# The last quad of a sliding-window attention step, its values loaded in two pieces in place of four

## The chip, the core and the metric

The kernel runs on one core of a Trainium2 chip. The metric is the device time of one execution in microseconds; three runs of the kernel before gave 186.46, 186.56 and 186.88, median 186.56.

## What is computed

One decoding step of attention for 32 sequences (B = 32, one token each). 32 query heads share 8 key/value heads (4 each), the head size is 128, and only the last 512 positions of a cache of 2048 are looked at. All inputs are bf16.

```
q = (x @ wq)                                  # 32 x 512 by 512 x 4096
k, v = last 512 rows of each cache, per (batch, kv head)
scores = q . k * 128**-0.5 ; p = softmax(scores)
o = p . v                                     # per (batch, head)
out = o.reshape(32, 4096) @ wo                # 4096 x 512
```

The keys and the values that are read are 33.5 MB each, wq and wo 4.2 MB each: 75.5 MB in all.

## The kernel before

**Tiling.** The batch is cut into eight quads of four sequences (q = 0 to 7). A quad's keys are one tile of 128 partitions by 32 KB: a partition is one (sequence, kv head, quarter of the window), its row 128 cache rows on end. The values of a quad have the same shape. There are two buffers each, `K_sb` and `V_sb`, used in turn by even and odd quads. At the start `V_sb[1]` holds wq; at the end `K_sb[0]` holds wo.

**Steps of a quad.** The texts `PE_OPS`, `DVE_OPS` and `ACT_OPS` (lines 19 to 33) give each engine its order of work by hand, one word for each step, and `needs` (lines 89 to 118) says what each step waits for. T turns the keys (VectorE, `KT_sb`, line 445); S makes the scores (TensorE, line 331); M, X and N are the softmax (VectorE and ScalarE); E brings the probabilities into the order of the value rows (TensorE, line 346) and G copies them out; B spreads them into a block-diagonal tile `bd` (ScalarE line 509, VectorE line 465). P multiplies by the values (TensorE, line 361): 32 groups of 4 matmuls, each group reading 512 columns of `V_sb`. `P7.0.32` in the order is all 32 groups of quad 7. C copies its result (VectorE line 470, ScalarE line 514), F folds it (line 373) and D writes it into `o_sel` (line 518). P of a quad waits for C of the quad before, F for C of its own. The end of TensorE's order is P6, F5, P7, F6, F7, and after D7 the projection by wo (line 393) in three blocks, one for each piece W0, W1, W2 of wo (16, 12 and 4 row groups); two copies each on VectorE and ScalarE and one store finish.

**Loads.** All large loads are issued by SyncE (SP) on one queue, in the order of the text `LOADS` (lines 35 to 37): K is a quad's keys in one piece, `Vq.i` is piece i of a quad's values, W the pieces of wo. `V_PIECES` (line 40) says into how many pieces the values of each quad are cut: 1 for quads 0 to 4, 2 for quads 5 and 6, 4 for quad 7. A piece takes its share of every partition's row, so whole tiles come in rows of 32 KB, halves in rows of 16 KB, quarters in rows of 8 KB. Each piece has a semaphore of its own. SP waits before the first piece of a quad's values (line 233) until P of the quad two before has ended, since it writes that buffer; the next pieces then follow without a wait. On TensorE `v_waits` (lines 178 to 184) puts a wait for a piece before the first group that reads it.

The lines that set this:

```
n = R // V_PIECES[q]                                  # line 234, R = 128
r0 = op[2] * n
sp.dma_start(V_sb[q % 2][:, r0 * DH:(r0 + n) * DH], rows(v_cache, q, r0, r0 + n)
...
n = V_PIECES[q]                                       # line 180, in v_waits
for i in range(n):
    if g0 <= i * 32 // n < g1:
        c = sum(1 for p in range(q % 2, q + 1, 2) if V_PIECES[p] > i)
        yield i * 32 // n, sem_v[q % 2][i], 16 * c
```

Of the kernel before, what the change touches and what calls it, by code (L numbers as in the profile page):

```python
# [32 lines left out]
"""  # L33

LOADS = """
K0 K1 V0.0 K2 V1.0 K3 V2.0 K4 V3.0 K5 K6 V4.0 K7 V5.0 V5.1 V6.0 V6.1 V7.0 V7.1 V7.2 V7.3 W0 W1 W2
""".split()

X_PARTS = [(0, 2), (2, 8), (8, 18), (18, 32)]
V_PIECES = [1, 1, 1, 1, 1, 2, 2, 4]  # L40
WOP = [(0, 16), (16, 28), (28, 32)]


# [4 lines left out]
def bass_standalone__sliding_block_cached__sampling_kernel(  # L48
# [71 lines left out]
    with ExitStack() as es:  # L120
# [46 lines left out]
        sem_k = [sem(f"sem_k{i}") for i in range(2)]  # L167
        sem_v = [[sem(f"sem_v{i}_{j}") for j in range(max(V_PIECES))] for i in range(2)]
        sem_wo = [sem(f"sem_wo{i}") for i in range(len(WOP))]
# [8 lines left out]
        def v_waits(q, g0, g1):  # L178

            n = V_PIECES[q]  # L180
# [4 lines that stand above are left out]
# [34 lines left out]
        def _(sp):  # L219
# [3 lines left out]
            for op in ops_of(" ".join(LOADS)):  # L223
# [5 lines left out]
                elif kind == "V":  # L229
                    if q == 1:  # L230
                        sp.wait_ge(s["pe_q"], 8)
                    if q >= 2:
                        wait([ends["P", q - 2, 31]])
                    n = R // V_PIECES[q]
                    r0 = op[2] * n
# [323 lines left out]
```

## Time and profile before

| what | us |
|---|---|
| median of three runs (186.46 to 186.88) | 186.56 |
| the profiled execution: its own time | 186.74 |
| its span, first to last instruction | 185.0 |
| TensorE busy with matmuls | 119.9 |
| VectorE busy | 106.5 |
| ScalarE busy | 49.7 |

The mean granted TensorE clock was 0.825 of full speed. The profile is of one execution. "Busy" is the time in which an engine had an instruction in work; "landing" is when a load's semaphore shows that all its bytes are there. All loads together moved 75.5 MB at a mean of 409 GB/s over the span. In the chain of waits each step is put down to what released the next, followed back from the end. In rows of the timeline the first two numbers are start and duration in us, x is the number of instructions, and the bracket gives the idle time of the engine before and what ended it.

### The profile page before, as it was taken

To read this page: it belongs to the slowest core of one execution; us is meant where nothing else is said; L and a number is where in the kernel's file an instruction comes from. 1 tells how busy PE (TensorE), PEld (TensorE's weight loads), DVE (VectorE), ACT (ScalarE), POOL (GpSimd) and SP (SyncE) were. 2 spreads that over 40 slices of the span, in tenths; PEclk is the share of its full clock that TensorE was granted. 3 is DMA by queue.
4 is the path that set the end of the run, shared out by engine and by line. 5 is a ranking of instruction groups with operands and counts; after the bars stand their busy time and mean duration, and the time that the engine had idled before them with its cause. 6 is when DMAs were issued, how large, how long until landed. Compare 5 with 4: busy or idle time off the path is not lost.

```text
span 185.0 us, 3664 instructions
## 1 busy us (share of the span) xinstructions
PE 119.9 (65%) x1636; PEld 56.3 (30%) x1636; DVE 106.5 (58%) x106; ACT 49.7 (27%) x93; POOL 16.9 (9%) x52
## 2 busy tenths in 40 slices
PE   0089104447696597649934994342799899898943
PEld 0024000013453153314421351001345446354542
DVE  0031999994549524972298328999637996320201
ACT  3000300012925037301650154001062715420301
POOL 7900040202000110001000200020000000000000
PEclk9999965556999799687995599655569999999996
DMA  6998999999999999999999999999999999999960
GB/s 213 421 500 369 432 454 454 454 390 404 450 454 443 411 386 454 454 436 425 392 436 454 432 418 411 439 446 439 418 411 411 429 425 425 411 420 431 431 287 27
DMA packets 3872, 75.80 MB, mean 410 GB/s; under 512 B 464, under 2 KB 528, under 8 KB 656
## 3 DMA queue, kind: packets, MB, share of 16 engines
q1 hardware_dynamic: 3792, 75.53, 95.9%
q8 instruction: 13, 0.21, 0.5%
q10 hardware_dynamic: 64, 0.03, 0.1%
q14 instruction: 3, 0.02, 0.0%
HBM read 75.53 MB, written 0.03 MB: 409 GB/s over the span
## 4 chain that ended last, share of the span: by engine, by line
DMA 59%; DVE 22%; PE 9%; issue 6%; SPq 2%; ACTq 1%; DVEq 0%
DMA K_sb<-in_k_cache_dram 43%; DVE KT_sb L445 17%; DMA K_sb<-in_wo_dram 12%; PE ps L313 4%; PE ps L361 4%; DMA bd<-in_x_dram 4%; DVE QT_sb L437 2%; DVE KT_sb L434 1%; SPq L236 1%; DVE C_sb L470 1%; ACTq L187 1%; SPq L242 1%; PE ps L331 1%; DVE bd L413 0%; PE ps L393 0%
## 5 line engine op out<-in xcount | busy, mean ns | idle before, releaser
L445 DVE STREAM_TRANSPOSE KT_sb<-K_sb 128x4096 f32<-128x4096 f32 x16 | 70.5, 4431 | 9.7 <-DMA K_sb<-in_k_cache_dram 9.6
L361 PE MATMUL ps<-V_sb,bd 32*128 32x512 bf16 x1024 | 64.1, 402 | 4.3 <-DMA V_sb<-in_v_cache_dram 1.7
L331 PE MATMUL ps<-KT_sb,QBD 128*32 128x512 bf16 x256 | 26.0, 544 | 39.0 <-DVE KT_sb L445 29.8
L361 PEld LDWEIGHTS ps<-V_sb,bd 32*128 32x128 bf16 x1024 | 27.4, 98 | 38.3 <-issue 14.7
L331 PEld LDWEIGHTS ps<-KT_sb,QBD 128*32 128x32 bf16 x256 | 6.7, 115 | 55.6 <-DVE KT_sb L445 36.9
L496 ACT ACTIVATE P_f<-ps,negmax 128x512 f32<-128x512 f32 x8 | 5.5, 687 | 62.3 <-DVE negmax L453 62.3
L509 ACT ACTIVATE bd<-PTc,mask 128x512 bf16<-128x512 bf16 x31 | 20.1, 711 | 0.3
L514 ACT ACTIVATE C_sb<-ps 32x512 f32<-32x512 f32 x22 | 12.9, 587 | 23.7 <-PE ps L361 23.5
L289 POOL COPY QBD<-QT_sb 32x128 bf16<-32x128 bf16 x32 | 9.2, 287 | 106.6 <-PE ps L331 89.9
L465 DVE TENSOR_SCALAR bd<-PTc,mask 128x512 bf16<-128x512 bf16 x33 | 9.3, 348 | 15.3 <-ACT PTc L503 15.3
L470 DVE COPY C_sb<-ps 32x512 f32<-32x512 f32 x10 | 6.9, 693 | 14.5 <-PE ps L361 14.4
L373 PE MATMUL ps<-C_sb,F_sb 128*128 128x128 f32 x64 | 9.7, 298 | 5.6 <-ACT C_sb L514 5.0
L373 PEld LDWEIGHTS ps<-C_sb,F_sb 128*128 128x128 f32 x64 | 8.2, 200 | 8.4 <-ACT C_sb L514 7.2
L346 PE MATMUL ps<-P_bf,E_sb 128*128 128x128 bf16 x128 | 9.8, 237 | 1.1 <-DVE P_bf L459 1.1
L451 DVE TENSOR_REDUCE maxv<-ps 128x1 f32<-128x512 f32 x8 | 5.5, 687 | 8.4 <-PE ps L331 8.4
L503 ACT ACTIVATE PTc<-ps 128x512 bf16<-128x512 f32 x8 | 4.7, 593 | 19.6 <-PE ps L346 19.6
L346 PEld LDWEIGHTS ps<-P_bf,E_sb 128*128 128x128 bf16 x128 | 8.3, 107 | 5.1 <-DVE P_bf L459 2.5
L313 PE MATMUL ps<-V_sb,bd 128*128 128x512 bf16 x32 | 9.1, 453 | 0.8 <-DVE bd L413 0.8
L301 PE MATMUL ps<-bd 32*128 32x128 bf16 x4 | 0.6, 295 | 8.9 <-DMA bd<-in_x_dram 8.9
L434 DVE CAST KT_sb<-ps 128x512 bf16<-128x512 f32 x4 | 2.5, 682 | 6.5 <-PE ps L313 6.5
L413 DVE CAST bd<-ps 128x512 bf16<-128x512 f32 x1 | 0.7, 692 | 9.5 <-PE ps L301 9.5
L490 ACT ACTIVATE KT_sb<-ps 128x512 bf16<-128x512 f32 x4 | 2.1, 603 | 14.3 <-PE ps L313 14.3
(29 smaller groups left out, 34.3 us busy)
## 6 DMA issues: line engine op xcount, KB each, us to landing
K_sb<-in_k_cache_dram SPq DMA_DIRECT2D x8, 4096.0 KB, 25.6
V_sb<-in_v_cache_dram SPq DMA_DIRECT2D x5, 4096.0 KB, 29.4
V_sb<-in_v_cache_dram SPq DMA_DIRECT2D x4, 2048.0 KB, 20.2
V_sb<-in_wq_dram SPq DMA_DIRECT2D x2, 2048.0 KB, 9.8
V_sb<-in_v_cache_dram SPq DMA_DIRECT2D x4, 1024.0 KB, 11.8
K_sb<-in_wo_dram SPq DMA_DIRECT2D x1, 2048.0 KB, 18.8
K_sb<-in_wo_dram SPq DMA_DIRECT2D x1, 1536.0 KB, 21.8
K_sb<-in_wo_dram SPq DMA_DIRECT2D x1, 512.0 KB, 22.6
```

The lines of the kernel that those rows point to most:

```text
L289: pool.tensor_copy(QBD[pr, q % 2].rearrange("p (w t) (h c) -> p w t h c", w=2, h=HKV)[:, :, :, :, 4 * b:4 * b + 4], QT_sb[pr, q].rearrange ...
L313: ins = pe.matmul(ps[:, n], lhsT=xT_sb[:, kt, :], rhs=wq_sb[:, kt, n * 512:(n + 1) * 512], start=kt == 0, stop=kt == DKT - 1, tile_positio ...
L331: ins = pe.matmul(S_ps[32 * c:32 * c + 32, :], lhsT=QBD[:, q % 2, 2 * w + t, c0:c0 + 32], rhs=KT_sb[:, w, :, KB * h:KB * h + KB, t], start ...
L346: ins = pe.matmul(EP_ps[:, e * R:(e + 1) * R], lhsT=E_sb[:, k, e].rearrange("p m j -> p (m j)"), rhs=P_bf[:, k * R:(k + 1) * R], start=k = ...
L361: ins = pe.matmul(O_ps[:, b, :], lhsT=bd[pr, q % 2, 4 * g:4 * g + 4].rearrange("p r h e -> p (r h e)"), rhs=V_sb[q % 2][pr, 512 * g:512 * ...
L373: ins = pe.matmul(F_ps[:, 0:P], lhsT=F_sb[:, d].rearrange("p h d -> p (h d)"), rhs=C_sb[:, q % 2, :, 32 * d:32 * d + 32], start=d == 0, st ...
L445: return dve.transpose(KT_sb[:, w].bitcast(F32).rearrange("p r c t -> p r (c t)"), K_sb[q % 2][:, :].bitcast(F32).rearrange("p (r w c) -> ...
L451: dve.tensor_reduce(maxv[:, q:q + 1], S_ps, AX.X, ALU.max).then_inc(s["dve_m"], 1)
L465: ins = dve.tensor_scalar(o, i, m, None, op0=ALU.mult)
L470: ins = dve.tensor_copy(*pick_args(q, r))
L509: ins = act.activation(o, i, ACTF.Copy, scale=m)
L514: ins = act.activation(*pick_args(q, r), ACTF.Copy)
```

## The change

The values of the last quad come in two pieces in place of four: `V_PIECES` ends in 2, and the words V7.2 and V7.3 leave the order of the loads. SP issues two DMAs of 2 MB (rows of 16 KB) where it issued four of 1 MB (rows of 8 KB). P7 has a wait before groups 0 and 16 where it had one before groups 0, 8, 16 and 24. As `sem_v` is made for the largest entry of `V_PIECES`, each of the two value buffers has two semaphores in place of four. All else is the same.

```
 LOADS = """
-K0 K1 V0.0 K2 V1.0 K3 V2.0 K4 V3.0 K5 K6 V4.0 K7 V5.0 V5.1 V6.0 V6.1 V7.0 V7.1 V7.2 V7.3 W0 W1 W2
+K0 K1 V0.0 K2 V1.0 K3 V2.0 K4 V3.0 K5 K6 V4.0 K7 V5.0 V5.1 V6.0 V6.1 V7.0 V7.1 W0 W1 W2
 """.split()
...
-V_PIECES = [1, 1, 1, 1, 1, 2, 2, 4]
+V_PIECES = [1, 1, 1, 1, 1, 2, 2, 2]
```

## The prediction

> **What bounds the kernel now.** I read the page first, its parts 1 to 3, to see which engine is full.
>
> ```profile
> span 185.0 us, 3664 instructions
> PE 119.9 (65%) x1636; PEld 56.3 (30%) x1636; DVE 106.5 (58%) x106; ACT 49.7 (27%) x93; POOL 16.9 (9%) x52
> DMA  6998999999999999999999999999999999999960
> ...
> q1 hardware_dynamic: 3792, 75.53, 95.9%
> q8 instruction: 13, 0.21, 0.5%
> ```
>
> No compute engine is above 65%; the 16 DMA engines are full from the second slice to the last but one. The kernel is a stream of 75.5 MB, and the end is set by when its last byte lands and by what must follow. So the next view is the end of the chain of waits (start, duration, what), and beside it the end of the timeline.
>
> ```profile
> 155.47 0.54 SPq L236
> 156.00 0.04 issue
> 156.04 0.60 SPq L236
> ...
> 158.62 0.43 SPq L242
> 159.05 0.04 issue
> 159.09 22.60 DMA K_sb<-in_wo_dram
> 181.69 0.04 issue
> ```
>
> ```profile
> 161.73 3.63 PE L361 MATMUL ps<-V_sb,bd 32*128 32x512 bf16 x64 [0.80 <-DMA V_sb<-in_v_cache_dram]
> 165.42 1.40 DVE L470 COPY C_sb<-ps 32x512 f32<-32x512 f32 x2 [6.70 <-PE ps L361]
> 167.07 7.09 PE L361 MATMUL ps<-V_sb,bd 32*128 32x512 bf16 x128 [0.62 <-DVE C_sb L470]
> 174.21 1.40 DVE L470 COPY C_sb<-ps 32x512 f32<-32x512 f32 x2 [7.39 <-PE ps L361]
> ...
> 177.33 1.08 PE L393 MATMUL ps<-K_sb,o_sel 128*32 128x128 bf16 x64 [0.37 <-ACT o_sel L518]
> 180.50 0.85 PE L393 MATMUL ps<-K_sb,o_sel 128*32 128x128 bf16 x48 [2.09 <-DMA K_sb<-in_wo_dram]
> 181.74 0.64 PE L393 MATMUL ps<-K_sb,o_sel 128*32 128x128 bf16 x16 [0.38 <-DMA K_sb<-in_wo_dram]
> ```
>
> The reader is to see three things. The last piece of wo (W2) lands at 181.69 and the last 16 matmuls start 0.05 later: this landing sets the end, with 3.3 us of fixed tail behind it (185.0 - 181.7). TensorE runs the value matmuls of the last quad (P7) from 167.07 without a break, started by the copy of P6 (165.42 + 1.40 = 166.82) and not by a load. And after the first block of the output projection, at 178.41, TensorE idles 2.09 us until W1 lands: the compute path has spare time there.
>
> Last, the landings. The semaphore events of the trace date them: V5.0 145.75, V5.1 150.65, V6.0 156.79, V6.1 161.69, V7.0 164.46, V7.1 166.94, V7.2 169.40, V7.3 171.90, W0 176.79, W1 180.46, W2 181.69. The view of DMA issues, asked for the issue at 155.47, the one at 157.34 and W0's at 157.98, and the stage sums say the same more coarsely:
>
> ```profile
> V_sb<-in_v_cache_dram SPq DMA_DIRECT2D x1, 1024.0 KB, 9.0
> V_sb<-in_v_cache_dram SPq DMA_DIRECT2D x1, 1024.0 KB, 14.6
> K_sb<-in_wo_dram SPq DMA_DIRECT2D x1, 2048.0 KB, 18.8
> ```
>
> ```profile
> 141.00:158.00 17.00, 16.40 (x268) 8.80 (x264) 14.76 (x17) 7.84 (x15) 0.00 (x0) 1.00 1.00 423
> 161.30:168.10 6.80, 5.75 (x92) 3.16 (x96) 1.39 (x2) 1.45 (x3) 0.00 (x0) 1.00 1.01 418
> ```
>
> The last columns are the granted clock, the DMA share and GB/s. In the first stretch only 16 KB rows move, in the second only 8 KB rows; both keep the engines full.
>
> **The change, part by part.** Everything up to 155.47, when SP's wait for P5 ends and V7.0 is issued, is untouched, so only the tail is costed.
>
> *Row size.* Two pieces of 16 KB rows replace four of 8 KB rows, the same 4 MB. Clean steps between landings: 2.48 and 2.46 and 2.50 us for 1 MB in 8 KB rows (164.46 to 171.90), mean 2.48; 4.90, 4.90 and 4.89 us for 2 MB in 16 KB rows (V5.0 to V5.1, V6.0 to V6.1, V7.3 to W0). So 4 x 2.48 = 9.92 becomes 2 x 4.90 = 9.80: -0.12. The rates agree: 4.194 MB take 10.03 us at 418 GB/s and 9.92 at 423, -0.11. Everything queued behind (W0, W1, W2) lands 0.12 earlier, as does the second half of V7 (171.78).
>
> *Two DMA issues fewer on SP.* Each took 0.60 us and 0.04 between: W0 to W2 are issued 1.28 us sooner. Costed at nothing: W0 is issued at 157.98, but followed packet by packet no DMA engine ends V7.3 before 168.15, so the issue has 10 us of cover. Nothing else is queued on SP until the output store. Were that cover gone the change would gain up to 1.28.
>
> *Two semaphore waits fewer in P7 on TensorE.* P7 waited at groups 0, 8, 16 and 24 and now waits at 0 and 16. None of the four showed idle time; 0.
>
> *The wait that becomes coarser.* First half: all 2 MB have to be there before group 0. They land where V7.1 did, 166.94 less half of 0.12, so 166.88, while P7 is held anyway until 167.07. About 0. Second half: group 16 is reached at 167.07 + 7.09/2 = 170.6 and its piece lands at 171.78, so TensorE waits 1.2 us; before, groups 16 and 24 needed their pieces at 170.6 and 172.4 and had them at 169.40 and 171.90. Behind this wait stand, on TensorE, 64 matmuls, two folds and the projection; on DVE and ACT the copies of P7. P6's second half shows the price: released by a landing at 161.69, started at 161.73, its copies begin 3.69 later. So the copies of P7 begin at 171.82 + 3.69 = 175.51 in place of 174.21: 1.30 late. The rest of that path shifts by as much: the projection's first block starts at 178.63 and ends at 179.71. W1 lands at 180.46 - 0.12 = 180.34: 0.63 still idle. If the path slipped further, W1's block of 0.85 would have to end by W2's landing at 181.57, so the first block could end at 180.72: the path is covered up to a slip of 1.01 more. Taken: 0. Bounds: below, the path cannot gain; above, 64 matmuls at half clock. The trace has 32 such matmuls in 3.44 us at a granted 0.50 (120 to 130), so 64 take 6.9 and not 3.63: +3.25, less the cover of 1.01, is +2.2. I take 0 since the granted clock was 1.00 from 137 to 181.6, through waits of 0.80 and 0.62.
>
> *The last 16 matmuls.* They took 0.64 for the clock fell to half at 181.57. At full clock, by the rows of 64 in 1.08 and 48 in 0.85 (0.0144 each), 16 take 0.39. With the change TensorE idles 0.63 and not 2.09 us shortly before, so the fall may not come: between 0 and -0.25. I take 0, because nothing says where the clock's steps fall in another run.
>
> The Trainium skill, "TensorE: Matmul & The Clock Gate", section Part 1, says that the clock is halved after an idle stretch judged in free-running windows of 3.4 us. By it the shorter idle time could spare the fall, and the sum would be -0.37 instead of -0.12. The trace's steps lie on a grid of 3.41 us, which agrees, but it shows one phase of that grid only.
>
> Sum: -0.12 + 0 + 0 + 0 + 0 = -0.12. The profiled execution took 186.74 (span 185.0 and 1.7 around it), 0.18 over the median of 186.56; it becomes 186.6, and the median **186.4**.
>
> **Rivals.** The runs before lie from 186.46 to 186.88; 0.2%, or 0.37 us, is about what can be told from no change.
>
> *B, the last block stays at full clock:* -0.12 - 0.25 = -0.37, 186.2. For it: the shorter idle time. Against it: it needs the median run to have had the fall before. It sits on the bound of 0.37.
>
> *C, the issues do count:* the chain of waits puts all four issues of V7 on the path. Two fewer and the shorter stream: -0.12 - 1.28 = -1.40, 185.2. Against it: W0 lands 4.89 after V7.3, a full engine's pace, so no engine waited for the issue.
>
> The Trainium skill, "DMA: Bandwidth & Descriptors", section Anatomy of one DMA, gives about 2 us fixed for each DMA plus its bytes at 436 GB/s, fitted on another path of issue; two DMAs fewer would be worth 4.0 us there, 182.6 by that estimate. The steps of 2.48 for 1 MB leave no room for a fixed 2 us between queued DMAs, so the trace does not agree.
>
> *D, slower, the coarse wait decides:* P7's second half comes more than 1.01 + 1.30 later than now, and then every further microsecond is one of the end. The price goes from 0 to the +2.2 above: 186.5 to 188.6. For it: two thirds of the present 2.09 us of idle time are used up. Against it: every duration in the sum is a measured row at the same clock.
>
> *E, slower, an instruction fetch more on the slowest engine:* V6.0 landed 6.14 after V5.1, not 4.90, since a 16 KB instruction packet (one of the 13 on q8) ran on that engine at 151.1. Followed packet by packet, one engine took 4.02 us over a megabyte in place of 2.48 when it was hit at 160.9, so a fetch costs its engine 1.5. At W2 four engines land 1.2 us or more behind the other twelve, and the last of them is the landing that counts. One fetch more on it: 186.4 + 1.5 = 187.9. Against it: the last four fetches before W2 (151.1, 160.9, 167.1, 175.7) each made another engine late and none a late one later, and TensorE's matmuls stay the same.
>
> **How the numbers follow.** Forecast 0.50, B 0.24, C 0.10, D 0.11, E 0.05. The forecast's own range is 186.2 to 186.7 (0 to -0.37, and the runs' spread). Outside the range stand C, E and D's upper half, 0.20 in all: it goes from 185.9 (B with the spread below) to 186.9 (D's lower part). Faster: C 0.10, two thirds of B 0.16, and 0.06 of the forecast, 0.32. Slower: D 0.10, E 0.05, 0.15. Within 0.2%: 0.53.
>
> **What would show it.** Right: V7.0 landing near 166.9 and V7.1 near 171.8; P7 in two blocks of 64 matmuls with an idle 1.2 us charged to the load of V between them; the wait before W1's block down from 2.09 to about 0.6; W2 landing near 181.6. Wrong: no wait before W1's or W2's block (D); landings of W0 to W2 earlier by about a microsecond (C); W2 later by 1.5 with P7 as forecast (E); the last block at 0.4 in place of 0.64 (B).

## The result, and the profile after

The changed kernel takes 186.44 us (median of 20 executions, 186.21 to 186.81). The kernel before, run beside it 20 times, takes 186.88 (186.46 to 187.59), 0.3 more than in the three runs shown ahead of the prediction. The ratio (its time over that of the kernel before beside it) is 0.9974, 95% interval 0.9964 to 0.9984: faster by 0.49 us, 0.30 to 0.67. The forecast was 186.4 and a gain of 0.12. The time and the sign came out, but the gain was four times the forecast; the rest of it lies in the spread of the kernel before.

The page of the changed kernel, parts 1 to 3 and the end of its chain of waits (start, duration, what):

```profile
span 184.7 us, 3662 instructions
...
DMA  6999999999999999999999999999999999999970
...
q1 hardware_dynamic: 3504, 75.53, 95.9%
```

```profile
155.66 0.54 SPq L236
156.20 0.04 issue
156.24 0.60 SPq L236
...
157.95 0.04 issue
157.99 23.64 DMA K_sb<-in_wo_dram
181.64 0.04 issue
```

Two issues fewer stand in the chain. The wait for W2 begins 1.1 us sooner (157.99, where it was 159.09), and W2 lands at 181.64, where it was 181.69: the earlier issue bought nothing, as the wait grew from 22.60 to 23.64. The timeline of the changed kernel's tail (start, duration, engine, operation; in brackets the idle time before it and what ended it; only the rows of the value matmuls and of the projection):

```profile
162.08 3.63 PE L361 MATMUL ps<-V_sb,bd 32*128 32x512 bf16 x64 [0.96 <-DMA V_sb<-in_v_cache_dram]
167.42 3.63 PE L361 MATMUL ps<-V_sb,bd 32*128 32x512 bf16 x64 [0.61 <-DVE C_sb L470]
171.88 3.63 PE L361 MATMUL ps<-V_sb,bd 32*128 32x512 bf16 x64 [0.83 <-DMA V_sb<-in_v_cache_dram]
...
178.69 1.08 PE L393 MATMUL ps<-K_sb,o_sel 128*32 128x128 bf16 x64 [0.37 <-ACT o_sel L518]
180.45 0.85 PE L393 MATMUL ps<-K_sb,o_sel 128*32 128x128 bf16 x48 [0.68 <-DMA K_sb<-in_wo_dram]
181.68 0.43 PE L393 MATMUL ps<-K_sb,o_sel 128*32 128x128 bf16 x16 [0.37 <-DMA K_sb<-in_wo_dram]
```

P7 is now two blocks of 64 matmuls. The second waits for its half of V7, the projection starts at 178.69 in place of 177.33, and the idle time before W1's block has shrunk from 2.09 to 0.68 us. The last block took 0.43 and not 0.64, as the clock fell only at 184.17 in this execution and at 181.57 in the profile before.

The stage sums over the same stretches as before show the rows (last column GB/s):

```profile
141.00:158.00 17.00, 15.96 (x260) 8.64 (x256) 14.64 (x16) 7.64 (x14) 0.00 (x0) 1.00 1.01 426
161.30:168.10 6.80, 5.40 (x88) 2.95 (x92) 1.39 (x2) 1.45 (x3) 0.00 (x0) 1.00 1.00 424
```

The second stretch moved 8 KB rows at 418 GB/s before and moves 16 KB rows at 424 now.

### The profile page after: what moved, and what is told of

The parts are those of the page before. It is cut to its first block, busy times and chain, and to the rows that moved or that the text cites. A ratio compares the mean times of both kernels' runs of the same rounds, so it can differ in the third digit from the quotient of the medians.

```text
span 184.7 us, 3662 instructions
## 1 busy us (share of the span) xinstructions
PE 119.1 (65%) x1636; PEld 56.8 (31%) x1636; DVE 106.6 (58%) x106; ACT 49.8 (27%) x93; POOL 16.9 (9%) x52
## 4 chain that ended last, share of the span: by engine, by line
DMA 77%; DVE 13%; issue 3%; PE 3%; SPq 3%; DVEq 0%
DMA K_sb<-in_k_cache_dram 49%; DMA V_sb<-in_v_cache_dram 15%; DMA K_sb<-in_wo_dram 13%; DVE KT_sb L445 12%; PE ps L361 2%; SPq L236 1%; SPq L228 1%; SPq L242 1%; PE ps L331 1%; SPq L193 0%; DVE C_sb L470 0%; DVE maxv L451 0%; PE ps L393 0%; DVEq L120 0%; DVE P_bf L479 0%
## 5 line engine op out<-in xcount | busy, mean ns | idle before, releaser
L361 PE MATMUL ps<-V_sb,bd 32*128 32x512 bf16 x1024 | 63.1, 397 | 4.7 <-DMA V_sb<-in_v_cache_dram 2.9
L331 PE MATMUL ps<-KT_sb,QBD 128*32 128x512 bf16 x256 | 25.3, 532 | 39.7 <-DVE KT_sb L445 30.0
L346 PE MATMUL ps<-P_bf,E_sb 128*128 128x128 bf16 x128 | 11.0, 255 | 0.8 <-DVE P_bf L459 0.8
L346 PEld LDWEIGHTS ps<-P_bf,E_sb 128*128 128x128 bf16 x128 | 9.3, 116 | 4.9 <-DVE P_bf L459 2.8
L313 PE MATMUL ps<-V_sb,bd 128*128 128x512 bf16 x32 | 8.5, 433 | 0.8 <-DVE bd L413 0.8
```

The costliest lines, as they stand in the source:

```text
L313: ins = pe.matmul(ps[:, n], lhsT=xT_sb[:, kt, :], rhs=wq_sb[:, kt, n * 512:(n + 1) * 512], start=kt == 0, stop=kt == DKT - 1, tile_positio ...
L331: ins = pe.matmul(S_ps[32 * c:32 * c + 32, :], lhsT=QBD[:, q % 2, 2 * w + t, c0:c0 + 32], rhs=KT_sb[:, w, :, KB * h:KB * h + KB, t], start ...
L346: ins = pe.matmul(EP_ps[:, e * R:(e + 1) * R], lhsT=E_sb[:, k, e].rearrange("p m j -> p (m j)"), rhs=P_bf[:, k * R:(k + 1) * R], start=k = ...
L361: ins = pe.matmul(O_ps[:, b, :], lhsT=bd[pr, q % 2, 4 * g:4 * g + 4].rearrange("p r h e -> p (r h e)"), rhs=V_sb[q % 2][pr, 512 * g:512 * ...
```

## The experiments

Two theories stood against each other at first. *Row theory:* all of the gain is the price of 8 KB rows and of two DMAs. *Clock theory:* 0.14 is that price, and the rest comes because TensorE's work lies 1.3 us later, idles less before W1, and keeps its clock for the last blocks. Every kernel was timed against the kernel before on the same chip; the experiments ran on three chips.

### The changed kernel again

Edit: none.

> The changed kernel itself, run beside the kernel before on the same chip as the next three. Both theories: about 0.4 to 0.5 us faster than before (20 runs gave 186.44 against 186.88). Clock theory: its times lie close together (within about 0.5 us), those of the kernel before spread by a microsecond, as the clock falls early, late or not at all in the 2.1 us in which TensorE idles before the second block of the projection.

Measured: 186.40 (12 executions, 186.27 to 186.55), the kernel before 186.67 (35 executions, 186.31 to 187.60), ratio 0.9985 (0.9974 to 0.9995). A gain of 0.28 by the ratio: just under the lower end of the first one, and less than the 0.4 to 0.5 that both theories expected. The spreads are as the clock theory said: the changed kernel's twelve lie within 0.3 us. Of the 35 of the kernel before, 26 lie from 186.31 to 186.80 and nine from 187.15 to 187.60, with nothing between. I call the latter *late* (187.0 or more).

### Only TensorE's timing changed

```diff
 # pv(): with four pieces of V7 as before
-pieces = {g: (sm, n) for g, sm, n in v_waits(q, g0, g1)}
+for g, sm, n in v_waits(q, g0, g1):   # quad 7: pieces 0, 1 before group 0; 2, 3 before group 16
+    pieces.setdefault(g - g % 16 if q == NQ - 1 else g, []).append((sm, n))
```

> The kernel before with four pieces of V7 and 8 KB rows kept, but P7 waits for its pieces as the changed kernel does: pieces 0 and 1 before group 0, pieces 2 and 3 before group 16. TensorE's work is moved later by 1.3 us and nothing else changes. Clock theory: 0.25 to 0.35 us faster than before, that is the gain less the 0.14 of the stream; the wait before the second block of the projection goes from 2.1 to about 0.7 us. Row theory: no change, within 0.1 us, or slower.

Its timeline:

```profile
171.81 3.63 PE L363 MATMUL ps<-V_sb,bd 32*128 32x512 bf16 x64 [1.04 <-DMA V_sb<-in_v_cache_dram]
...
180.28 0.85 PE L395 MATMUL ps<-K_sb,o_sel 128*32 128x128 bf16 x48 [0.58 <-DMA K_sb<-in_wo_dram]
181.51 0.43 PE L395 MATMUL ps<-K_sb,o_sel 128*32 128x128 bf16 x16 [0.38 <-DMA K_sb<-in_wo_dram]
```

Measured: 186.55 (12 executions, 186.30 to 186.70), ratio 0.9990 (0.9979 to 1.0000). A gain of 0.12 by the medians and 0.19 by the ratio, where 0.25 to 0.35 was expected, with an interval that reaches no change; but not one of the twelve is late, against nine of 35 beside it. At that rate a dozen without a late one has a chance of 3%. So coarser waits on the same loads seem to be enough to remove the late executions, which speaks against rows or the number of DMAs as their source. What still separates this kernel from the changed one on the same chip is 186.55 to 186.40, or 186.54 to 186.41 in the means: 0.13 to 0.15, the rows and the two DMAs.

### The idle time filled, twice

```diff
 # after the first block of the projection (j == 0)
+for g in range(8):                    # first form
+    pe.matmul(EP_ps[0:32, :], lhsT=o_sel[:, g, :], rhs=V_sb[0][:, 512 * g:512 * g + 512], ...)
```
```diff
+for g in range(8):                    # second form: as the value matmuls, 4 row groups
+    for b4 in range(4):
+        pe.matmul(O_ps[:, b4, :], lhsT=bd[pr, 0, 4 * g:4 * g + 4]..., rhs=V_sb[0][pr, 512 * g:512 * g + 512], ...)
```

> The kernel before with four pieces of V7 kept, and eight matmuls of no use (32x512 into a free PSUM bank, about 0.22 us each at full clock) put behind the first block of the projection, to fill the 2.1 us in which TensorE idles there. Clock theory (the change gains 0.14 by the stream, and the rest, some 0.3, because TensorE no longer idles long enough before the last blocks for its clock to fall): 0.25 to 0.35 us faster than before, last block about 0.43 in place of 0.64, and times that lie close together. Row theory (all of the gain comes from fewer DMAs and longer rows): no faster than before, within 0.1 us.

> The changed kernel with two such matmuls of no use behind the first block of the projection, where it still idles 0.7 us. Clock theory: the clock holds there already, so within 0.1 us of the changed kernel. Row theory: the same as the changed kernel.

> The kernel before, and behind the first block of the projection 32 matmuls of no use in the form of the value matmuls (four row groups, 512 columns; 64 of them took 3.63 us at full clock, so 1.8 us), which fill the 2.1 us of idle time with the kind of work that the clock is known to hold through. Clock theory: the group of executions above 187.1, a quarter of those of the kernel before, is gone, and the median is 0.05 to 0.2 lower than before; the eight matmuls of the earlier try, which used a quarter of the array, did not count as work. Rival (the late executions come from the loads or from an instruction fetch): the group above 187.1 stays.

Measured, first form: 186.58 (186.44 to 188.27), ratio 1.0012 (0.9990 to 1.0035). Eight of twelve lie from 186.44 to 186.60, but four are late (187.08 to 188.27). Three of these four take 2.6 to 2.7 us more than their span, where 1.8 is usual, as in only one late execution of the kernel before (188.00, below); the added matmuls may have brought something of their own. The same work in the changed kernel, two matmuls only: 186.40 (186.27 to 186.58), ratio 0.9978 (0.9964 to 0.9992), as the changed kernel itself. Second form: 186.49, ten of twelve from 186.27 to 186.56, two late (187.38 and 187.61); ratio 0.9987 (0.9969 to 1.0004), with ten late ones among 23 of the kernel before beside it. So the bulk did become narrow, and the one trace of each shows a clock that held through the projection (it fell at 184.65 with the first form, at 185.94 with the second). The second form:

```profile
178.37 1.91 PE L405 MATMUL ps<-V_sb,bd 32*128 32x512 bf16 x32
180.43 0.85 PE L393 MATMUL ps<-K_sb,o_sel 128*32 128x128 bf16 x48
181.67 0.43 PE L393 MATMUL ps<-K_sb,o_sel 128*32 128x128 bf16 x16 [0.39 <-DMA K_sb<-in_wo_dram]
```

Late executions did not all go. The clock theory, which put the whole of them down to that idle time, missed; but two of twelve against ten of 23 are too few to tell whether the filling removed some of them. That the first form's matmuls do not count as work for the clock, as was supposed for the second, is not shown either: the clock held in its trace.

### What a fallen clock costs in the tail

```diff
 # SP, between W0 and W1
+wait([ends["P", NQ - 2, 31]])
+sp.dma_start(V_sb[0][:, 64 * DH:128 * DH], rows(v_cache, 6, 64, 128)).then_inc(sem_junk, 16)
```

The second kernel has this and 112 matmuls of the second form in the idle time.

> The kernel before with a load of 2 MB of no use between W0 and W1, so that TensorE idles 7 us and not 2.1 before the second block of the projection. All loads behind it land 4.9 us later, so 191.5 at least. Clock theory: the clock has fallen when W1 lands; the blocks of 48 and of 16 matmuls take about 1.5 and 0.64 us in place of 0.85 and 0.43, the second block ends after W2 has landed (0.85 of room grows too small: 1.23 between the two landings), and the span ends 0.4 to 0.6 later after W2's landing than with a held clock. Rival: the tail behind W2's landing stays at 3.0 to 3.3 us.

> The same, with 112 matmuls of no use (6.2 us at full clock) in the idle time. Clock theory: the blocks take 0.85 and 0.43, 0.4 to 0.6 us faster than without them. Rival: no difference within 0.15 us.

The timeline without the filling matmuls, and with them:

```profile
177.57 1.08 PE L399 MATMUL ps<-K_sb,o_sel 128*32 128x128 bf16 x64 [0.37 <-ACT o_sel L524]
185.36 1.90 PE L399 MATMUL ps<-K_sb,o_sel 128*32 128x128 bf16 x64 [6.71 <-DMA K_sb<-in_wo_dram]
```

```profile
179.06 6.22 PE L411 MATMUL ps<-V_sb,bd 32*128 32x512 bf16 x112
185.85 0.85 PE L399 MATMUL ps<-K_sb,o_sel 128*32 128x128 bf16 x48 [0.57 <-DMA K_sb<-in_wo_dram]
187.09 0.43 PE L399 MATMUL ps<-K_sb,o_sel 128*32 128x128 bf16 x16 [0.38 <-DMA K_sb<-in_wo_dram]
```

In the first the clock fell at 182.58, in the idle time, and both blocks run on end in 1.90 us. The span ends 3.30 us after W2's landing (189.84 less 186.54) and 3.05 with the held clock (190.09 less 187.04). So the cost of the clock is real, but in these two traces, even fallen for both blocks, it is 0.25 and not 0.4 to 0.6. The times: 191.64 (191.46 to 191.69), and with the filling 191.36, 191.42, 192.73 and 192.98. Two are 0.25 better as the mechanism says, two over a microsecond worse. The traced one, 192.98, has an instruction fetch that starts at 192.33, after its last instruction (190.1): its time is 2.9 us over its span, where 1.8 is usual. The run of 192.73 has the usual 1.8 and a span of 190.9, so that is not its cause.

### The dose of 8 KB rows doubled

```diff
-V_PIECES = [1, 1, 1, 1, 1, 2, 2, 2]
+V_PIECES = [1, 1, 1, 1, 1, 4, 4, 2]
```

> The changed kernel, with the values of quads 5 and 6 in four pieces of 8 KB rows each in place of two of 16 KB: twice the dose of what the change took away, the other way round, at a place where TensorE's waits do not set the end. Stream theory (each quad of 8 KB rows costs 0.12 to 0.14 us more): 0.24 to 0.28 us slower than the changed kernel, about 186.65. Row theory (the whole 0.3 to 0.5 of the change is the price of 8 KB rows and more DMAs): 0.6 to 1.0 slower, 187.0 or more.

Measured: 186.60 (186.53 to 187.30, one of twelve late), ratio to the kernel before 0.9995 (0.9982 to 1.0008). That is 0.16 to 0.20 over the changed kernel's medians (186.44 and 186.40, from the comparisons above) for two quads: a little under the stream theory's 0.24 to 0.28, far from the row theory's 0.6 to 1.0. The row theory falls. Its trace shows a second thing:

```profile
167.22 8.78 PE L361 MATMUL ps<-V_sb,bd 32*128 32x512 bf16 x128 [2.04 <-DMA V_sb<-in_v_cache_dram]
```

Here P6 ended sooner and TensorE idled 2.04 us ahead of P7. The clock was at half from 168.12 to 171.53, P7 took 8.78 in place of 7.09, and it ran in one block, without a pause before group 16. The idle time behind the projection's first block, 0.34 us, was what was left of the cover. So two pieces alone do not keep every execution from being late; the late one itself was not traced.

### One piece

```diff
-V_PIECES = [1, 1, 1, 1, 1, 2, 2, 2]
+V_PIECES = [1, 1, 1, 1, 1, 2, 2, 1]
```

> The changed kernel with the values of the last quad in one piece of 32 KB rows, the next step in the same direction. By the steps of the prediction: the loads land another 0.05 to 0.1 us earlier, V7 near 171.7; P7 then runs from 171.7 for 7.1 us without cover, the copies start at 178.9 in place of 175.5, the projection's first block at 182.1, after all of wo has landed, and the three blocks run on end in about 1.9 us to 184.0 where the last ended at 182.1: 1.9 us slower than the changed kernel, 188.2 to 188.5. The rival that the coarse wait costs nothing: 186.3.

Measured: 190.51 (190.14 to 191.18), ratio 1.0179 (1.0129 to 1.0229): slower than the changed kernel by 4.1 us, where 1.9 was expected. Timeline and stage sums (the column ahead of the last two is the granted clock):

```profile
171.68 9.10 PE L361 MATMUL ps<-V_sb,bd 32*128 32x512 bf16 x128 [5.17 <-DMA V_sb<-in_v_cache_dram]
```

```profile
171.60:176.00 4.40, 4.32 (x44) 1.91 (x48) 0.00 (x0) 0.00 (x0) 0.00 (x0) 0.52 0.99 421
176.00:181.00 5.00, 5.00 (x94) 2.54 (x83) 0.17 (x1) 0.17 (x1) 0.00 (x0) 1.00 0.57 236
```

V7 landed where it was expected (171.55, forecast 171.7), but in the 5.17 us of waiting the clock fell (168.97) and came back only at 175.80: P7 took 9.10 and not 7.09. The rest of the miss in this execution is the output store, which took 2.1 us to land and not 1.5:

```profile
out_dram<-P_bf SPq DMA_DIRECT2D x1, 32.0 KB, 2.1
```

The thirteenth instruction fetch started at 186.68 and lasted 0.96, into the store's packets (187.48 to 187.88). One of the store's 16 completion events is at 188.67, all others by 188.12.

### Late executions of the kernel before: two traces, the spans and a shifted fetch

> The kernel before once more, for the trace of one of its late executions (187.0 and above, a third of them), which the changed kernel has none of. Clock theory: in a late one TensorE's clock is at half before W1 lands at about 180.5, and the blocks of 48 and 16 matmuls run on end in about 1.9 us as in the run with the long gap; W2 lands at 181.6 to 181.8 all the same, and the span ends 0.3 to 0.6 later behind it. Load theory: W2 itself lands 0.4 to 0.9 later than 181.7, since one DMA engine was hit once more, and the tail behind it keeps its 3.0 to 3.3 us.

> The same again: a late execution shows by one look in three. What each theory expects is as for the look before.

Neither execution was late (186.36 and 186.38, while four of the seven beside them were, 187.10 to 188.00). No late one of the kernel before was traced. What the two do show is the kernel before when its clock holds. The second's timeline:

```profile
177.51 1.08 PE L393 MATMUL ps<-K_sb,o_sel 128*32 128x128 bf16 x64 [0.37 <-ACT o_sel L518]
180.37 0.85 PE L393 MATMUL ps<-K_sb,o_sel 128*32 128x128 bf16 x48 [1.78 <-DMA K_sb<-in_wo_dram]
181.59 0.43 PE L393 MATMUL ps<-K_sb,o_sel 128*32 128x128 bf16 x16 [0.37 <-DMA K_sb<-in_wo_dram]
```

The clock fell at 182.32 here, after the last block, at 181.84 in the first (last block 0.46), and at 181.57 in the profile ahead of the prediction (0.64). After W2's landing the span takes 3.05 in the first of these traces, 3.05 in the second and 3.26 in that profile.

The late ones have no trace, but the span of every execution beside the experiments is on record. Of these 82 of the kernel before 28 are late. Their spans are 185.1 to 185.6, those of the others 184.5 to 185.0. The time outside the span is 1.75 to 2.0 in 27 of the 28 and 2.7 in the one of 188.00. So most of the lateness lies within the span, and a fetch that starts after the program's end, as in the run of 192.98, can be behind one of them at most. The mean granted clock (0.814 in the late ones, 0.815 in the others) does not tell them apart.

The last experiment tests whether the late ones are meetings of fetch and store, as in the run with one piece.

```diff
 # before the first scores of quad 0
+for _ in range(64):
+    pe.matmul(Y_ps[0:32, 0:32], lhsT=QBD[:, 0, 0, 0:32], rhs=KT_sb[:, 0, 0:32, 0, 0], ...)
```

> The kernel before with 64 matmuls of no use (32 columns each) at the start, in 2.4 us in which TensorE idles before the second scores of quad 0. They lie far from the tail and hide nothing there; they only make TensorE's program 128 instructions longer, so that every fetch of 16 KB of its instructions comes half a block earlier in the kernel: the thirteenth, which starts at 181.4 to 182.1 and in the run with one piece of V7 ran into the output store (2.1 us to land in place of 1.5), comes at about 178, and the next would come after the end. Fetch theory (the late executions of the kernel before, 32 of 85 so far at 187.0 or more, are those in which the last fetch meets the output store): none or one of twelve is late, the median falls to about 186.5 and the output store lands after 1.5 us. Clock theory (they come from the clock falling in the 2.1 us of idle time before W1): four or five of twelve are late, as before, and the median is unchanged.

Measured: 186.74 (186.41 to 187.09), the kernel before 186.61 (186.37 to 187.38) with five late ones of 17, at 187.24 to 187.38; ratio 0.9997 (0.9982 to 1.0013). Its thirteenth fetch did come at 179.36, in the one trace. Nothing lies above 187.09, but two of twelve are still late (187.06 and 187.09) and the median did not fall. Neither theory's numbers came out, and two of twelve against five of 17 decide nothing. (Of the 85 executions of the kernel before up to then 31 were late by the bound of 187.0, not 32.)

## Why the prediction was right in its time and short in its gain

**Row size: right.** The term was -0.12. W2's landing less V6.1's, taken on the eighth of the 16 DMA engines to land so that the engines hit by instruction fetches do not count, is 19.69 to 19.74 in the seven traces with four pieces and this placing of loads (the kernel before three times, coarse waits, both fillings, the shifted fetch) and 19.57 to 19.60 in four with two pieces: 0.14. The time between coarse waits and the changed kernel, 0.13 to 0.15, says the same without a trace. On the slowest engine, which sets the end, the same difference is 19.68 to 20.00 and 19.58 to 19.94: there single late engines blur it.

**Two issues fewer: right at nothing.** V7.1 landed at 171.84 and W0 at 176.74, 4.90 apart, as before (4.89); rival C is refuted.

**The coarser wait: right.** Second block at 171.88 (forecast 171.82), projection at 178.69 (178.63), idle before W1 0.68 (0.63). The wait between the halves was 0.83 and not 1.2, as P7 itself began 0.35 later in this execution. Rival D had its price in the run with one piece: there the cover is gone, and the fallen clock that bounded D added 2.0 us to P7.

**The last 16 matmuls and one time for the kernel before: the step that fell short.** In the sum only the last 16 matmuls, "I take 0", depended on the execution, and the kernel before stood as one time, that of three runs from 186.46 to 186.88. Over all its executions beside these experiments and the result (102), 36 took 187.0 or more; of the changed kernel's 44 (two matmuls of no use added in twelve) none did. The 65 of the kernel before up to 186.92 have a mean of 186.58, the 44 a mean of 186.43: 0.15, the rows. All 102 have a mean of 186.84. So of 0.41 in the means, 0.15 is the stream, which the sum had, and 0.26 the late executions, which it had not. (Of the 55 that ran beside the changed kernel alone 17 were late; there the two shares are 0.18 and 0.22.) TensorE's later timing seems to remove them: with the coarse waits alone none of twelve was late.

**The time of 186.4: in part luck.** It starts from 186.56, the median of three runs of which none was late; with 36 late ones in 102 that has a chance of 27%. Beside the result the kernel before took 186.88, from which the same working would have given 186.8. So the start was 0.32 too low and the gain 0.37 too small, and the two nearly cancel.

**Rival B named the place but not the size.** The clock falls behind the 2.09 us of idle time, at 181.57, 181.84 and 182.32 in the three traces of the kernel before, and where it fell ahead of the last block the tail was 0.21 longer (3.26 against 3.05). The 0.25 that B took was worked out with 0.39 for 16 matmuls at full clock; they take 0.43. With both blocks at half clock, in the run with the long gap, it cost 0.25. Most late executions lie 0.5 to 0.9 above the mean of the others, so a clock that falls there does not by itself make one. **Rival E** did not come: W2 landed at 181.64, not 1.5 later.

**What stays open:** what makes an execution of the kernel before late. None of 56 executions was late of the kernels whose traces show a pause in the value matmuls of quad 7 before group 16 (the changed kernel's 44, the coarse waits' twelve); late ones still came when the idle time behind the projection's first block was filled. A last instruction fetch that meets the output store (0.55 us, one trace) is of the right size and lies within the span, as most of the lateness does, but it was seen in another kernel, and the run that moved the fetch away gave a mixed answer. A later landing of W2 is untested too, as no late execution has a trace.

None of the variants beat the changed kernel; with two filling matmuls it has the same 186.40 as on its own beside them.

## What to carry to other kernels

Between loads that are queued on end, count only bytes and row length: an issue saved ahead of a 10 us backlog was worth nothing here, though the chain of waits puts the issues on its path, and 8 KB rows in place of 16 KB cost 1.4% of their own stretch. Where a change is worth less than the spread of the kernel, get that spread from some twenty executions of both first: the gain here lay more in the late executions that went than in the path that was worked out. A wait may be made coarser as long as the work behind it keeps idle time before the next wait; with one piece the cover was gone, and the longer wait also brought the clock down.

## What the runs showed that was not expected

- Moving TensorE's work 1.3 us later, with nothing saved, narrowed the spread of the times: 186.30 to 186.70 in twelve executions, where the kernel before had 186.31 to 187.60 in 35. The clock is not the whole of it, as a fallen one was worth 0.25 us in the runs with the long gap. The Trainium skill, "TensorE: Matmul & The Clock Gate", section Part 1, has the clock fall after an idle window and come back after a busy one. The run with one piece agrees (5.17 us idle, half clock from 168.97 to 175.80).
- An idle time of 2.04 us ahead of P7 was enough for the clock to fall for 3.41 us in one trace (quads 5 and 6 in four pieces); P7 took 1.7 us longer there, and the cover before W1 hid it.
- A fetch of TensorE's instructions, 16 KB on one DMA engine, lasted 0.9 to 1.3 us and made that engine's next megabyte 1.5 us late (4.02 in place of 2.48); near the end it met the output store once, and one of the store's completion events came 0.55 us behind the others.
- After a long wait P7 ran 2.0 us longer than its full-clock time, so that one piece cost 190.51 where 188.2 to 188.5 was worked out.
